# Blockwise causal attention and a ReGLU feed-forward on one core: packed loads and DMA transposes for batches 2 and 3, stores from the ACT queue, a shorter order for batch 0

## The chip, the cores and the metric

The kernel runs on one NeuronCore of a Trainium2 chip. TensorE (PE in the profile) multiplies matrices, VectorE (DVE) and ScalarE (ACT) work on elements, GpSimd (POOL) does so too and issues DMAs, and SyncE (SP) only issues DMAs here. The metric is the device time of one execution in microseconds (us). Ratios are the mean time of one kernel's fast runs over that of the other's fast runs of the same rounds, so they are not quite the ratio of the medians that are quoted. A profile is one execution; its span is about 2 us shorter than the time reported for that execution.

## The reference, cut to what matters

```python
q, k, v: (8 batches, 8 heads, 576 positions, 64), float32
scores = q @ k.T / 8,  masked where block_i < block_j (blocks of 64 positions)
attn   = softmax(scores) @ v
x      = attn with the heads side by side: (8 * 576, 512)
out    = (relu(x @ w_gate) * (x @ w_val)) @ w_out     # d_ff = 1536
```

## The kernel before: the parts that matter

The work is cut into 32 head pairs, r = 0 to 31, four to a batch. For each pair, TensorE makes scores, ACT takes the exponential, TensorE multiplies with v ("av"), and DVE normalises the result into `xnat`. `xnat` is then transposed into `xT`, the input of the feed-forward. The feed-forward is a generator. `ffn(n)` emits its next n matmuls, and these fill the gaps of the attention of later batches. The kernel fixes the order of the instructions of each engine itself, and an instruction that waits holds up those that stand after it in that order.

Batches 0, 1 and 2 are loaded as float32 in packed form (4 x 64 consecutive numbers for a partition), cast to bf16 and transposed by TensorE. The evacuation from PSUM undoes the packing. Batches 3 to 7 are loaded by casting DMAs from POOL and transposed by the DMA engines, with SP issuing the transposes. Stores go out on SP.

```python
def load_qkv(b, which):                       # batches 3 to 7
    ...
            nc.gpsimd.dma_start(dst, src[b, :, 128 * c : 128 * c + n, :].rearrange("h p d -> p h d"))

def dma_transposes(b):
    m, tl = bfs[b, 0], bfs[b, 1]
    for t in range(2):
        nc.sync.dma_start_transpose((qTm, kTm)[t][b % 2]..., m[t]...)
        nc.sync.dma_start_transpose((qTt, kTt)[t][b % 2][:, 0:4, :], tl[t])
...
                ob = sb.tile([128, 512], FP, name="ob", bufs=3)      # end of an output group of ffn
                nc.vector.tensor_copy(ob, op)
                if j < B:
                    r0 = S * j + 128 * s
                    nc.sync.dma_start(out[r0 : r0 + 128, :], ob)
...
        for r in range(4, 4 * B):
            b, hp = divmod(r, 4)
            a = {1: [2, 6, 2, 4], 2: [4, 8, 4, 8]}.get(b, [4, 8, 8, 16])
            ...
            exp_2 = scores_1(r)
            ffn(a[0])
            exp_2()
            if r > 4:
                head_av(r - 1, 0)
                ffn(a[1])
                head_av(r - 1, 1)
                ...                             # xnat transposes: TensorE up to r = 8, DMA after
            if hp == 0 and 2 <= b < B - 1:
                load_qkv(b + 1, (0, 1, 2))
            if hp == 2 and 2 <= b < B - 1:
                dma_transposes(b + 1)
            ffn(a[2])
            scores_2(r)
            scores_3(r)
            if r < 7:
                pe_transposes(1, (r + 1) % 4, e1.m, e1.tl, (dve, dve))
            elif r < 11:
                pe_transposes(2, (r + 1) % 4, e2.m, e2.tl, (dve, dve))
            ffn(a[3])
            corners(r, nc.vector)
```

The softmax here doesn't subtract the row's maximum and nothing guards it: scores larger than these inputs give would overflow.

## Time and profile before

| what | us |
|---|---|
| time, median of the first three runs | 410.58 |
| span of the profiled execution | 406.5 |
| feed-forward begins | 33.10 |
| first scores of batch 3 | 127.30 |
| rest, batch 3 to the end | 279.2 |

The three stretches that these moments bound, in the view by windows of the kernel before. The columns are each engine's busy time with its instruction count, then the granted TensorE clock, the DMA share and the GB/s moved:

```profile
core 0: us, PE busy (x) PEld busy (x) DVE busy (x) ACT busy (x) POOL busy (x), PEclk, DMA share, GB/s
0.00:33.10 33.10, 24.87 (x284) 13.75 (x285) 16.22 (x56) 17.58 (x27) 14.53 (x33) 0.95 1.13 218
33.10:127.30 94.20, 77.20 (x685) 38.16 (x684) 48.20 (x130) 40.59 (x64) 26.73 (x31) 0.95 1.06 148
127.30:406.50 279.20, 274.32 (x2058) 131.07 (x2058) 114.49 (x282) 110.95 (x166) 41.93 (x50) 0.99 0.63 80
```

The last stretch is full, so what can be gained lies before 127.3 us. The longest waits of TensorE in the kernel before, as total, number of times and longest one:

```profile
PE sc L236 <- DMA kTm_89<-k_bf: 9.0, 1, 9.0
PE ffnp L322 <- DVE xnat L305: 4.0, 5, 0.9
PE ffnp L403 <- POOL ident masks.py:199: 1.8, 1, 1.8
PE ffnp L220 <- DVE q_bt L153: 1.7, 1, 1.7
```

The first line is one wait, for the DMA transpose of batch 3's keys. SP issued that transpose at 115.65 us and it landed 11.6 us later. The granted clock is 0.53 between 120 and 130 us. SP's timeline has it (start, duration of the issue, what):

```profile
115.65 5.91 SPq L189 DMA_TRANSPOSE kTm_89<-k_bf  x1
```

### The profile page before, as it was taken

To read this page: it belongs to the slowest core of one execution; us is meant where nothing else is said; L and a number is where in the kernel's file an instruction comes from. 1 tells how busy PE (TensorE), PEld (TensorE's weight loads), DVE (VectorE), ACT (ScalarE), POOL (GpSimd) and SP (SyncE) were. 2 spreads that over 40 slices of the span, in tenths; PEclk is the share of its full clock that TensorE was granted. 3 is DMA by queue.
4 is the path that set the end of the run, shared out by engine and by line. 5 is a ranking of instruction groups with operands and counts; after the bars stand their busy time and mean duration, and the time that the engine had idled before them with its cause. 6 is when DMAs were issued, how large, how long until landed. Compare 5 with 4: busy or idle time off the path is not lost.

```text
span 406.5 us, 7570 instructions
## 1 busy us (share of the span) xinstructions
PE 376.4 (93%) x3024; PEld 183.0 (45%) x3024; DVE 178.9 (44%) x468; ACT 169.1 (42%) x257; POOL 83.2 (20%) x114
## 2 busy tenths in 40 slices
PE   6789898879964999999999999999999999999995
PEld 2444344534432444444445444444444444444442
DVE  2653565476531344444543444344434542433432
ACT  5563255535442345534553555355435511311310
POOL 5710211831340830092019002100000000000000
PEclk9989989999995999999999999999999999999998
DMA  8999996997398996299629962918031012002004
GB/s 206 244 203 240 199 261 169 115 117 59 33 152 82 108 184 103 60 137 175 118 29 172 142 126 31 151 42 131 18 103 32 16 40 77 2 26 79 0 9 95
DMA packets 144274, 43.54 MB, mean 107 GB/s; under 512 B 127856, under 2 KB 139632, under 8 KB 144240
## 3 DMA queue, kind: packets, MB, share of 16 engines
q0 software_dynamic: 76128, 13.57, 44.4%
q1 hardware_dynamic: 68112, 29.51, 32.5%
q8 instruction: 23, 0.38, 0.4%
q14 instruction: 11, 0.09, 0.1%
HBM read 37.75 MB, written 9.44 MB: 116 GB/s over the span
## 4 chain that ended last, share of the span: by engine, by line
PE 83%; DVE 7%; DMA 4%; issue 1%; SPq 1%; ACT 1%; POOL 1%; DVEq 0%; ACTq 0%
PE ffnp L357 23%; PE ffnp L373 22%; PE ffnp L345 22%; PE sc L236 7%; PE av L295 7%; DMA kTm_89<-k_bf 3%; DVE xnat L305 1%; DVE qTm_86 L221 1%; DMA stage<-in_k_dram 1%; PE ffnp L217 1%; DVE hT L367 1%; PE ffnp L322 1%; DVE k_bf L145 1%; DVE q_bf L145 1%; DMA k_bf<-in_k_dram 1%
## 5 line engine op out<-in xcount | busy, mean ns | idle before, releaser
L367 DVE TENSOR_TENSOR hT<-gate_sb,ffnp 128x512 bf16<-128x512 bf16 x108 | 74.2, 687 | 117.5 <-PE ffnp L357 84.2
L354 ACT ACTIVATE gate_sb<-ffnp 128x512 bf16<-128x512 f32 x108 | 64.3, 595 | 86.3 <-PE ffnp L345 85.4
L373 PEld LDWEIGHTS <-hT 128*128 128x128 bf16 x432 | 39.0, 98 | 43.5 <-issue 1.7
L383 DVE COPY ob<-ffnp 128x512 f32<-128x512 f32 x36 | 24.9, 691 | 59.5 <-PE ffnp L373 57.6
L373 PE MATMUL ffnp<-wo_85,hT 128*128 128x512 bf16 x144 | 37.4, 380 | 0.0
L373 PE MATMUL ffnp<-wo_84,hT 128*128 128x512 bf16 x144 | 37.3, 379 | 0.0
L373 PE MATMUL ffnp<-wo_83,hT 128*128 128x512 bf16 x144 | 37.2, 380 | 0.0
L261 ACT ACTIVATE attnT_95<-sc 128x1024 bf16<-128x1024 f32 x16 | 16.4, 1026 | 35.6 <-PE sc L236 31.6
L305 DVE TENSOR_TENSOR xnat<-av,recip 128x320 bf16<-128x320 f32 x60 | 29.5, 492 | 2.1
L251 ACT ACTIVATE attnT_94<-sc 128x1024 bf16<-128x1024 f32 x16 | 16.4, 1025 | 32.8 <-PE sc L236 24.4
L357 PE MATMUL ffnp<-xT,wv_82 128*128 128x512 bf16 x96 | 26.6, 400 | 0.0
L261 ACT ACTIVATE attnT_94<-sc 128x1024 bf16<-128x1024 f32 x16 | 16.4, 1024 | 23.9 <-PE sc L236 23.9
L251 ACT ACTIVATE attnT_95<-sc 128x1024 bf16<-128x1024 f32 x16 | 16.4, 1025 | 23.2 <-PE sc L236 22.0
L345 PE MATMUL ffnp<-xT,wg_78 128*128 128x512 bf16 x96 | 25.2, 383 | 0.3 <-DVE hT L367 0.3
L357 PE MATMUL ffnp<-xT,wv_81 128*128 128x512 bf16 x96 | 24.7, 380 | 0.4 <-DVE qTt_90 L225 0.4
L357 PE MATMUL ffnp<-xT,wv_79 128*128 128x512 bf16 x96 | 24.7, 380 | 0.4 <-DVE qTt_90 L225 0.4
L357 PE MATMUL ffnp<-xT,wv_80 128*128 128x512 bf16 x96 | 24.7, 379 | 0.4 <-DVE qTt_90 L225 0.4
L345 PE MATMUL ffnp<-xT,wg_75 128*128 128x512 bf16 x96 | 24.8, 379 | 0.0
L179 POOL DMA_DIRECT2D v_bf_97<-in_v_dram x15 | 12.6, 856 | 59.5 <-PE av L295 53.1
L345 PE MATMUL ffnp<-xT,wg_76 128*128 128x512 bf16 x96 | 24.7, 380 | 0.0
L345 PE MATMUL ffnp<-xT,wg_77 128*128 128x512 bf16 x96 | 24.7, 380 | 0.0
L295 PEld LDWEIGHTS <-attnT_95 128*128 128x128 bf16 x480 | 19.4, 101 | 10.6 <-DVE xnat L305 2.1
(115 smaller groups left out, 452.1 us busy)
## 6 DMA issues: line engine op xcount, KB each, us to landing
out_dram<-ob SPq DMA_DIRECT2D x32, 256.0 KB, 2.9
stage<-in_v_dram SPq DMA_DIRECT2D x27, 128.0 KB, 5.3
q_bf<-in_q_dram POOLq DMA_DIRECT2D x20, 128.0 KB, 6.3
k_bf<-in_k_dram POOLq DMA_DIRECT2D x20, 128.0 KB, 8.0
stage<-in_q_dram SPq DMA_DIRECT2D x4, 512.0 KB, 5.2
stage<-in_k_dram SPq DMA_DIRECT2D x4, 512.0 KB, 6.2
v_bf_97<-in_v_dram POOLq DMA_DIRECT2D x12, 128.0 KB, 5.1
stage<-in_q_dram SPq DMA_DIRECT2D x4, 256.0 KB, 4.1
```

The costliest lines, as they stand in the source:

```text
L179: nc.gpsimd.dma_start(dst, src[b, :, 128 * c : 128 * c + n, :].rearrange("h p d -> p h d"),)
L236: nc.tensor.matmul(o, kTm[b % 2][ps, c, hp, :] if c < 4 else kTt[b % 2][ps, hp : hp + 2, :].rearrange("p h n -> p (h n)"), qTm[b % 2][ps, ...
L251: nc.scalar.activation(at[:, :, 0:512], sc, AF.Exp, scale=scale)
L261: nc.scalar.activation(at[:, :, 1024:1536], sc, AF.Exp, scale=scale)
L295: nc.tensor.matmul(av[:, p, :], at[:, hh, col : col + 128], vb[:, c, h, :], start=(p == 0), stop=(c == p), skip_group_check=True,)
L305: nc.vector.tensor_tensor(out=xnat[:, :, 64 * hh : 64 * hh + 64], in0=av[:, :, 0:64], in1=recip.to_broadcast([128, NCH, 64]), op=AX.mult,)
L345: nc.tensor.matmul(gate, wg[i][:, c, fo : fo + 128], x[:, c, :], start=(c == 0), stop=(c == 3),)
L354: nc.scalar.activation(gate_sb, gate, AF.Relu)
L357: nc.tensor.matmul(val, wv[i][:, c, fo : fo + 128], x[:, c, :], start=(c == 0), stop=(c == 3),)
L367: nc.vector.tensor_tensor(out=h, in0=gate_sb, in1=val, op=AX.mult)
L373: nc.tensor.matmul(op, hT[f][:, 128 * s : 128 * (s + 1)], wo[f // 4][:, f % 4, :], start=(f == 0), stop=(f == 11),)
L383: nc.vector.tensor_copy(ob, op)
```

## The change: intent and diff

The change makes batch 3's operands early, so that the 9 us wait goes. It also takes transposes off TensorE. Batch 3 gets packed loads too. Batches 2 and 3, and the second half of batch 1, are transposed by DMA into a buffer `perm`, and a copy undoes the packing. POOL does the casts of batches 2 and 3. The 48 matmuls `ffn(8)+ffn(8)+ffn(32)` stand before batch 2. The loads of w_out come later, and those of q and k from batch 4 on earlier. Stores move to ACT and are issued one output group late. Batch 0's loop is reordered.

```diff
+        def transpose(self, hg):
+            for t in range(2):
+                pm = sb.tile([128, 4, 2, 128], BF, name="perm", bufs=8)
+                nc.sync.dma_start_transpose(pm..., self.m[t][:, 1024 * hg : 1024 * hg + 1024])
+        def unpermute(self, hp, engs):          # perm -> qTm, kTm
+            for t in range(2):
+                engs[t]((qTm, kTm)[t][self.b % 2][:, :, hp, :]..., self.perm[t, hp // 2]...)
...
+    def put(j, s, ob):
+            nc.scalar.dma_start(out[r0 : r0 + 128, :], ob)
...
-                    nc.sync.dma_start(out[r0 : r0 + 128, :], ob)
+                if store:
+                    store.pop()()
+                store.append(lambda j=j, s=s, ob=ob: put(j, s, ob))
...
-            a = {1: [2, 6, 2, 4], 2: [4, 8, 4, 8]}.get(b, [4, 8, 8, 16])
+            a = {1: [2, 4, 2, 4], 2: [4, 4, 4, 4]}.get(b, [4, 8, 8, 16])
             if r == 8:
+                head_av(7, 0)
+                ffn(8)
+                head_av(7, 1)
+                ffn(8)
+                to_xT_pe(7)
+                e2.unpermute(0, (dve, pool))
+                ffn(32)
...
+            elif r == 6:
+                e2.transpose(0)
+                e2.transpose(1)
+                e2.transpose_tails()
+                e3 = Early(3, 4)
+                e3.load_qk(0)
+                e3.load_qk(4)
+                e3.load_v(0)
+                e3.load_v(4)
+            elif r == 8:
+                e2.cast_v(0, pool)
+                e2.cast_v(4, pool)
+                e3.cast_qk(0, (pool, pool))
+                e3.cast_qk(4, (pool, pool))
+                e3.transpose(0)
+                e3.transpose(1)
+                e3.transpose_tails()
+            if 8 <= r < 11:
+                e2.unpermute(r - 7, (dve, pool if r == 8 else dve))
+            elif 11 <= r < 15:
+                e3.unpermute(r - 11, (dve, dve))
+            if r == 11:
+                for h0 in (0, 4):
+                    e3.cast_v(h0, pool)
```

(Cut: batch 0's loop; batch 1's start; the loads of q and k from batch 4 on; later places for the transposes of `xnat`; shapes of views.)

More of the change, by code (lines that the diff above doesn't have):

```diff
@@ L90, in new_bf @@
     def new_bf():
-        m = [sb.tile([128, 4, 512], BF, name=n, bufs=2) for n in ("q_bf", "k_bf")]
+        m = [sb.tile([128, 2048], BF, name=n, bufs=2) for n in ("q_bf", "k_bf")]
         t = [sb.tile([64, 512], BF, name=n, bufs=2) for n in ("q_bt", "k_bt")]
@@ L105, in __init__, with load_qk @@
             self.st = {}
-        def load(self, h0, gate=None):
+            self.perm = {}
+        def load_qk(self, h0, gate=None):
             b, per = self.b, self.per
@@ L123, in load, with load_v @@
                 both = new_stage(1024)
-                self.st_t = [both[:, 0:512], both[:, 512:1024], new_stage(512)]
+                self.st_t = [both[:, 0:512], both[:, 512:1024], None]
                 self.tail(0, q)
                 self.tail(1, k)
+            return i
+        def load_v(self, h0, gate=None):
+            b, per = self.b, self.per
             st = self.st[2, h0] = new_stage(256 * per)
             for h in range(per):
-                nc.sync.dma_start(
+                i = nc.sync.dma_start(
                     st[:, 256 * h : 256 * h + 256].rearrange("p (c d) -> p c d", c=4),
@@ L132, in load @@
                 )
+                after(i, gate)
             if h0 == 0:
+                self.st_t[2] = new_stage(512)
                 self.tail(2, v)
@@ L140, in tail, with half, cast_qk @@
             )
-        def cast_qk(self, h0, engs):
+        def half(self, t, hg):
+            return self.m[t][:, 1024 * hg : 1024 * hg + 1024].rearrange(
+                "p (j n) -> p j n", j=4
+            )
+        def cast_qk(self, h0, engs, tails=True):
             per = self.per
+            lo = 64 * (h0 % 4)
             for t in range(2):
                 engs[t](
-                    self.m[t][:, :, 64 * h0 : 64 * (h0 + per)].rearrange(
+                    self.half(t, h0 // 4)[:, :, lo : lo + 64 * per].rearrange(
                         "p j (h d) -> p h j d", d=64
@@ L150, in cast_qk, with cast_tails @@
                 )
-            if h0 == 0:
-                for t in range(2):
-                    engs[t](self.tl[t], self.st_t[t][0:64])
+            if h0 == 0 and tails:
+                self.cast_tails(engs)
+        def cast_tails(self, engs):
+            for t in range(2):
+                engs[t](self.tl[t], self.st_t[t][0:64])
         def cast_v(self, h0, eng):
@@ L165, in cast_v, with transpose_tails, pe_mains, pe_tails @@
                 )
+        def transpose(self, hg):
+            for t in range(2):
+                pm = sb.tile([128, 4, 2, 128], BF, name="perm", bufs=8)
+                nc.sync.dma_start_transpose(
+                    pm.rearrange("p j h n -> p (j h) n"),
+                    self.m[t][:, 1024 * hg : 1024 * hg + 1024],
+                )
+                self.perm[t, hg] = pm
+        def transpose_tails(self):
+            for t in range(2):
+                nc.sync.dma_start_transpose(
+                    (qTt, kTt)[t][self.b % 2][:, 0:4, :], self.tl[t]
+                )
+        def unpermute(self, hp, engs):
+            for t in range(2):
+                engs[t](
+                    (qTm, kTm)[t][self.b % 2][:, :, hp, :].rearrange(
+                        "p c (n j) -> p c n j", j=4
+                    ),
+                    self.perm[t, hp // 2][:, :, hp % 2, :].rearrange(
+                        "p j (c n) -> p c n j", c=4
+                    ),
+                )
+        def pe_mains(self, hp, evac):
+            for t in range(2):
+                tp = psum_ffn.tile([128, 512], BF, name="ffnp")
+                src = self.half(t, hp // 2)
+                lo = 128 * (hp % 2)
+                for j in range(4):
+                    nc.tensor.transpose(
+                        tp[:, 128 * j : 128 * j + 128], src[:, j, lo : lo + 128], ident
+                    )
+                evac[t](
+                    (qTm, kTm)[t][self.b % 2][:, :, hp, :].rearrange(
+                        "p c (n j) -> p c n j", j=4
+                    ),
+                    tp.rearrange("p (j c n) -> p c n j", j=4, c=4),
+                )
+        def pe_tails(self, evac):
+            tp = psum_ffn.tile([128, 2, 4, 64], BF, name="ffnp")
+            for t in range(2):
+                for hp in range(4):
+                    nc.tensor.transpose(
+                        tp[:, t, hp, :],
+                        self.tl[t][:, 128 * hp : 128 * hp + 128],
+                        ident[:64, :64],
+                    )
+            for t in range(2):
+                evac[t]((qTt, kTt)[t][self.b % 2][:, 0:4, :], tp[:, t])
     def load_qkv(b, which):
@@ L176, in load_qkv @@
                         bfs[b, 0], bfs[b, 1] = new_bf()
-                    dst = bfs[b, 0][t][:, c, :] if c < 4 else bfs[b, 1][t]
+                    dst = bfs[b, 0][t][:, 512 * c : 512 * c + 512] if c < 4 else bfs[b, 1][t]
                     dst = dst.rearrange("p (h d) -> p h d", h=8)
@@ L190, in dma_transposes @@
                 (qTm, kTm)[t][b % 2].rearrange("p c h n -> p (c h) n"),
-                m[t].rearrange("p c n -> p (c n)"),
+                m[t],
             )
@@ L209, in load_w_out @@
         return after(ins, gate)
-    def pe_transposes(b, hp, m, tl, evac):
-        hs = slice(128 * hp, 128 * hp + 128)
-        for t in range(2):
-            tp = psum_ffn.tile([128, 1024], BF, name="ffnp")
-            for j in range(4):
-                nc.tensor.transpose(
-                    tp[:, 128 * j : 128 * j + 128], m[t][:, j, hs], ident
-                )
-            nc.tensor.transpose(tp[:, 512:576], tl[t][:, hs], ident[:64, :64])
-            evac[t](
-                (qTm, kTm)[t][b % 2][:, :, hp, :].rearrange("p c (n j) -> p c n j", j=4),
-                tp[:, 0:512].rearrange("p (j c n) -> p c n j", j=4, c=4),
-            )
-            evac[t]((qTt, kTt)[t][b % 2][:, hp, :], tp[:, 512:576])
     def scores(b, hp, pieces):
@@ L273, in corners @@
         at = attnT[r % 2]
-        for c in (0, 512, 896, 1024):
-            eng.memset(at[64:128, :, c : c + 64], 0.0)
+        three = at[64:128, :, 0:1536].rearrange("p g (c n) -> p g c n", c=3)
+        eng.memset(three[:, :, :, 0:64], 0.0)
+        eng.memset(at[64:128, :, 896:960], 0.0)
     xnats = {}
@@ L334, in to_xT_dma @@
         nc.sync.dma_start_transpose(xTt[:, hp, b : b + 1, :], xnat[0:64, 4, :])
+    store = []
+    def put(j, s, ob):
+        if j < B:
+            r0 = S * j + 128 * s
+            nc.scalar.dma_start(out[r0 : r0 + 128, :], ob)
+        else:
+            for i in range(2):
+                r0 = S * (2 * s + i) + 512
+                nc.scalar.dma_start(out[r0 : r0 + 64, :], ob[64 * i : 64 * i + 64])
     def ffn_gen():
@@ L383, in ffn_gen @@
                 nc.vector.tensor_copy(ob, op)
-                if j < B:
-                    r0 = S * j + 128 * s
-                    nc.sync.dma_start(out[r0 : r0 + 128, :], ob)
-                else:
-                    for i in range(2):
-                        r0 = S * (2 * s + i) + 512
-                        nc.sync.dma_start(out[r0 : r0 + 64, :], ob[64 * i : 64 * i + 64])
+                if store:
+                    store.pop()()
+                store.append(lambda j=j, s=s, ob=ob: put(j, s, ob))
                 yield
@@ L410 @@
         for h0 in range(0, 8, 2):
-            e0.load(h0)
+            e0.load_qk(h0)
+            e0.load_v(h0)
         junk(12)
-        e0.cast_qk(0, (dve, act))
-        pe_transposes(0, 0, e0.m, e0.tl, (dve, act))
-        e0.cast_qk(2, (dve, dve))
-        for h0 in range(0, 4, 2):
-            e0.cast_v(h0, pool)
+        e0.cast_qk(0, (dve, act), tails=False)
+        e0.pe_mains(0, (dve, act))
+        e0.cast_tails((dve, dve))
+        e0.cast_v(0, pool)
+        e0.cast_v(2, pool)
         w_in = [load_w_in(i) for i in range(4)]
-        w_out = [load_w_out(i) for i in range(3)]
-        e1 = Early(1, 4)
         for r in range(4):
-            scores_1(r)()
+            exp_2 = scores_1(r)
+            if r == 0:
+                e0.pe_tails((dve, dve))
+            exp_2()
+            if r > 0:
+                head_av(r - 1, 0)
             if r < 3:
-                pe_transposes(0, r + 1, e0.m, e0.tl, (dve, dve))
+                e0.cast_qk(2 * r + 2, (dve, dve))
+                e0.pe_mains(r + 1, (dve, dve))
             if r > 0:
-                corners(r - 1, nc.vector)
-                head_av(r - 1, 0)
-            if r < 2:
-                e0.cast_qk(2 * r + 4, (dve, dve))
+                head_av(r - 1, 1)
+            junk(2)
+            scores_2(r)
+            scores_3(r)
+            junk(3)
+            if r > 0:
+                to_xT_pe(r - 1)
             if 1 <= r < 3:
                 e0.cast_v(2 * r + 2, dve)
-            junk(2)
-            scores_2(r)
-            if r > 0:
-                head_av(r - 1, 1)
-            scores_3(r)
-            junk(2)
-            if r > 0:
-                to_xT_pe(r - 1)
-        e1.load(0, w_in[2])
-        e1.load(4)
-        corners(3, nc.vector)
+            corners(r, nc.vector)
+        e1 = Early(1, 4)
+        e1.load_qk(0, w_in[2])
+        e1_qk = e1.load_qk(4)
         head_av(3, 0)
@@ L446 @@
         to_xT_pe(3)
-        e2 = Early(2, 4)
-        ffn(64)
-        e1.cast_qk(0, (dve, dve))
+        ffn(52)
+        w_out = [load_w_out(i, e1_qk) for i in range(3)]
+        e1.load_v(0)
+        e1.load_v(4)
+        e1.cast_qk(0, (dve, act))
+        ffn(8)
+        e1.pe_mains(0, (dve, dve))
+        e1.pe_tails((dve, act))
+        e1.cast_qk(4, (dve, act))
+        e1.transpose(1)
+        e2 = Early(2, 4)
+        e2.load_qk(0)
+        e2.load_qk(4)
+        e2.load_v(0)
+        e2.load_v(4)
+        ffn(8)
+        e1.pe_mains(1, (dve, dve))
         e1.cast_v(0, pool)
@@ L452 @@
         ffn(8)
-        pe_transposes(1, 0, e1.m, e1.tl, (dve, dve))
-        e2.load(0, w_out[1])
-        e2.load(4)
-        ffn(4)
         for r in range(4, 4 * B):
             b, hp = divmod(r, 4)
-            a = {1: [2, 6, 2, 4], 2: [4, 8, 4, 8]}.get(b, [4, 8, 8, 16])
+            a = {1: [2, 4, 2, 4], 2: [4, 4, 4, 4]}.get(b, [4, 8, 8, 16])
             if r == 8:
-                for h0 in (0, 4):
-                    e2.cast_qk(h0, (dve, dve))
+                head_av(7, 0)
+                ffn(8)
+                head_av(7, 1)
+                ffn(8)
+                to_xT_pe(7)
+                e2.unpermute(0, (dve, pool))
+                ffn(32)
             exp_2 = scores_1(r)
@@ L465 @@
             exp_2()
-            if r > 4:
+            if r in (4, 8):
+                ffn(a[1])
+            else:
                 head_av(r - 1, 0)
@@ L469 @@
                 head_av(r - 1, 1)
-                if r <= 8:
-                    to_xT_pe(r - 1)
-                else:
+                if r > 8:
                     to_xT_dma(r - 1)
-            else:
-                e1.cast_qk(4, (dve, dve))
-                ffn(a[1])
-            if r == 8:
-                for h0 in (0, 4):
-                    e2.cast_v(h0, pool)
-            if hp == 0 and 2 <= b < B - 1:
-                load_qkv(b + 1, (0, 1, 2))
-            if hp == 2 and 2 <= b < B - 1:
-                dma_transposes(b + 1)
+            if r == 4:
+                e1.unpermute(2, (pool, pool))
+                e1.unpermute(3, (pool, pool))
+                e2.cast_qk(0, (pool, pool))
+                e2.cast_qk(4, (pool, pool))
+            elif r == 6:
[20 more added lines that the diff above has]
+            if r == 11:
+                for h0 in (0, 4):
+                    e3.cast_v(h0, pool)
+            if b >= 2 and hp == 2 and b + 2 < B:
+                load_qkv(b + 2, (0, 1))
+            if b >= 3 and b + 1 < B:
+                if hp == 0:
+                    load_qkv(b + 1, (2,))
+                if hp == 2:
+                    dma_transposes(b + 1)
             ffn(a[2])
+            if 4 < r < 8:
+                to_xT_pe(r - 1)
             scores_2(r)
             scores_3(r)
-            if r < 7:
-                pe_transposes(1, (r + 1) % 4, e1.m, e1.tl, (dve, dve))
-            elif r < 11:
-                pe_transposes(2, (r + 1) % 4, e2.m, e2.tl, (dve, dve))
             ffn(a[3])
@@ L497 @@
         ffn(10**6)
+        store.pop()()
 _INS = ['q', 'k', 'v', 'moe_w_gate', 'moe_w_val', 'moe_w_out']
```

## The prediction

> **What bounds the kernel now.** TensorE. It is busy 376.4 of 406.5 us (busy table), 83% of the chain that ended last. But the three parts of the span differ (windows and TensorE timeline):
> - 0 to 33.1 us, attention of batch 0: 24.9 us busy, latency bound. A head pair takes 4.8 to 7.3 us; DVE and TensorE take turns.
> - 33.1 to 127.3 us: feed-forward matmuls of four take 0.866 us (0.2165 each); one head pair's attention costs about 2.0 us, as (39.24 us period of a batch later - 144 x 0.2165)/4. By these this part holds 228 x 0.2165 + 8 x 2.0 + 6 us of transposes = 71 us of work, and takes 94. The waits: 9.0 us in one piece at 118 to 127 for the DMA transpose of batch 3's keys (landed 11.6 us after issue), 4.0 us before the transposes of xnat, 1.7 us on a cast, 1.3 us on evacuations (0.42 us each). The granted clock is halved for 3.4 us twice before 60 us and for 10 us around the long wait (0.53 between 120 and 130). The Trainium skill ("TensorE: Matmul & The Clock Gate", Part 1) says that an idle window of about 3.4 us halves the clock; this trace agrees.
> - 127.3 us to the end: full (201.8 of 202 us busy, then tail). Nothing to gain there.
>
> **What the change does.**
> 1. Batch 3 is loaded early in packed form and cast on Pool, so the 9.0 us wait goes, and with it about 1.8 us of half clock.
> 2. 56 fewer TensorE transposes: about 3 us at 0.055 us each. Evacuations of 0.69 + 0.18 us per tensor leave DVE; SBUF copies (estimated 0.35 to 0.6 us, from the 128x512 casts' 0.41 to 0.62) come in.
> 3. Fillers replace waits: xnat transposes come later, 48 feed-forward matmuls stand before batch 2. 236 instead of 228 are done before batch 3: 1.7 us less afterwards.
> 4. Shorter batch 0: tails off the first chain (0.8 us), head 0's av before the next transposes, one fewer evacuation per tensor: 3 us in all, feed-forward starts near 30 us.
> 5. Stores on ACT, a group late: SP no longer holds loads behind stores. Worth little by itself.
>
> **New costs.** w_out now is asked for after batch 1's q and k (about 37 us); 3 MB took 13 us in before under similar load, and it is needed near 53 us: 0 to 3 us wait. Batch 2's second key copy stands on Pool behind batch 3's casts, whose loads stand on SP behind batch 2's transposes (1.9 to 3.8 us issue for 128x2048): 2 to 5 us wait in batch 2's second head pair. Between the two av of a pair only 4 matmuls (0.87 us) remain against a normalising of about 1.0 us: 0.2 us x 7.
>
> **Sum.** 30 + 71 + about 9 of waits to the start of batch 3 (110 us), then 1060 x 0.2165 + 20 x 2.0 + 4.7 tail = 275 us: span 385. Times stand 2 to 4 us over the span: 388 us, range 380 to 397. Nearly all is on the critical path. Faster 0.95, same 0.04, slower 0.01.
>
> **What would show it.** Feed-forward start near 30; batch 3's first scores near 110 with no long DMA wait; the period after that still 39.2 us per batch; the largest new wait at batch 2's second head pair, on Pool.
>
> **What would make it wrong.** Pool or w_out much later than estimated , or ACT stores delaying Relu in the full part.

## The result, and the profile after

The changed kernel takes 396.01 us (median of 4 runs, 395.18 to 397.32) against 410.17 us for the kernel before on the same chip. The ratio is 0.966, with a 95% interval of 0.962 to 0.970. That lies inside the predicted range of 380 to 397, close to its upper end. The central forecast of 388 was 8 us too good: a gain of about 22 us was expected and 14 came.

The same three stretches in the view by windows of the changed kernel:

```profile
core 0: us, PE busy (x) PEld busy (x) DVE busy (x) ACT busy (x) POOL busy (x), PEclk, DMA share, GB/s
0.00:31.30 31.30, 23.49 (x283) 13.77 (x288) 15.82 (x44) 16.71 (x25) 12.41 (x30) 0.95 1.15 221
31.30:117.50 86.20, 73.08 (x624) 35.22 (x635) 41.71 (x85) 43.28 (x69) 35.70 (x40) 0.98 1.33 201
117.50:393.90 276.40, 269.41 (x2012) 129.52 (x2049) 117.35 (x250) 109.90 (x166) 42.22 (x50) 1.00 0.72 82
```

The first stretch is 1.8 us shorter, the second 8.0 us and the last 2.8 us. In the last, 1.7 us are the 8 matmuls that are now done earlier. The middle stretch was forecast at 80 us, from 30 to 110, and took 86.2. TensorE's longest waits in the changed kernel:

```profile
PE ffnp L217 <- DVE q_bf L159: 3.8, 3, 1.3
PE ffnp L427 <- ACT gate_sb L424: 2.9, 1, 2.9
PE sc L294 <- DVE kTm_88 L202: 2.1, 1, 2.1
PE ffnp L469 <- POOL ident masks.py:199: 1.8, 1, 1.8
PE ffnp L217 <- DVE hT L437: 1.4, 1, 1.4
PE av L354 <- DVE xnat L364: 1.4, 3, 0.5
```

The 9 us wait is gone. Two new waits stand near the place of batch 2, and neither is the one that was forecast.

**The first of them: ACT stands behind a store.** ACT's instructions around 82 us in the changed kernel, from the timeline (start, duration, what; in brackets the idle time before, and what ended it):

```profile
80.20 0.58 ACT L383 COPY xT<-ffnp 128x512 bf16<-128x512 bf16 x1 [5.16 <-PE ffnp L382]
80.68 0.22 ACT L384 COPY xTt<-ffnp 128x64 bf16<-128x64 bf16 x1
85.61 0.34 ACTq L401 DMA_DIRECT2D out_dram<-ob  x1
85.99 1.09 ACT L424 ACTIVATE gate_sb<-ffnp 128x512 bf16<-128x512 f32 x2 [5.09 <-DMA stage<-in_k_dram]
```

The store at 85.61 writes an output tile that DVE had finished at 78.34. What ended ACT's wait was a load of keys. On POOL, the cast of that key load begins at 85.68, which is the same moment (POOL's timeline):

```profile
85.68 1.04 POOL L159 CAST k_bf<-stage 128x1024 bf16<-128x1024 f32 x1 [1.36 <-DMA stage<-in_k_dram]
```

Every Relu of the feed-forward stands behind this store on ACT, so TensorE waits 2.9 us (83.7 to 86.6 us), and its clock is halved for 3.4 us after that (86.8 to 90.3 us). In the compiled program each DMA from SP or ACT, but for the first eight, waits first for one of eight completion counters, which SP and ACT share in turn. The lines for that store and for the last DMA before it that holds the same counter (from the list of compiled instructions, not the profile):

```
SP   DMACopy stage_1039<-in_k_dram 128x4x256 [waits DMAHW3_49]
ACT  DMACopy out_0_dram<-ob_1215 128x512     [waits DMAHW3_49,DVE_49]
```

So a store on ACT waits for the landing of an unrelated load that SP issued. This is the first theory to test.

**The second: a copy of 3.09 us.** DVE near 102 us in the changed kernel, from the timeline:

```profile
101.28 3.09 DVE L202 COPY qTm_86<-perm 128x512 bf16<-128x512 bf16 x1
104.30 0.58 DVE L202 COPY kTm_88<-perm 128x512 bf16<-128x512 bf16 x1
```

POOL at the same time:

```profile
101.26 1.12 POOL L174 CAST v_bf_97<-stage 128x1024 bf16<-128x1024 f32 x1
102.25 0.69 POOL L179 CAST v_bf_97<-stage 64x512 bf16<-64x512 f32 x1
102.80 1.12 POOL L174 CAST v_bf_97<-stage 128x1024 bf16<-128x1024 f32 x1
```

Two copies of one form take 3.09 and 0.58 us. The long one spans three POOL casts and ends 0.45 us after the last of them. The Trainium skill ("SBUF — State Buffer", section "SBUF: two separate sides") says that DVE and GpSimd share a pair of SBUF ports as an exclusive lock, held for a whole instruction. This is the second theory.

### The profile page after: what moved, and what is told of

It reads as the page before. It is cut to its first block, busy times and chain, and to the rows that moved or that the text cites. A ratio compares the mean times of both kernels' runs of the same rounds, so it can differ in the third digit from the quotient of the medians.

```text
span 393.9 us, 7338 instructions
## 1 busy us (share of the span) xinstructions
PE 366.0 (93%) x2918; PEld 178.5 (45%) x2972; DVE 174.9 (44%) x378; ACT 169.9 (43%) x259; POOL 90.3 (23%) x120
## 4 chain that ended last, share of the span: by engine, by line
PE 74%; issue 2%; ACT 2%; DVE 2%; DMA 2%; SPq 1%; ACTq 0%; DVEq 0%
PE ffnp L443 22%; PE ffnp L427 21%; PE ffnp L415 19%; PE av L354 6%; PE sc L294 6%; DMA stage<-in_k_dram 2%; DVE xnat L364 1%; ACT attnT_94 L319 1%; ACT attnT_95 L319 1%; DVE hT L437 1%; ACT gate_sb L424 1%; SPq L196 0%; DVE ob L453 0%; DVE recip L363 0%; SPq L117 0%
## 5 line engine op out<-in xcount | busy, mean ns | idle before, releaser
L443 PE MATMUL ffnp<-wo_84,hT 128*128 128x512 bf16 x139 | 36.6, 380 | 0.3
L443 PE MATMUL ffnp<-wo_83,hT 128*128 128x512 bf16 x139 | 35.9, 379 | 0.4
L443 PE MATMUL ffnp<-wo_85,hT 128*128 128x512 bf16 x133 | 35.1, 380 | 0.4
L427 PE MATMUL ffnp<-xT,wv_79 128*128 128x512 bf16 x96 | 25.6, 390 | 2.9 <-ACT gate_sb L424 2.9
L415 PE MATMUL ffnp<-xT,wg_75 128*128 128x512 bf16 x95 | 25.6, 390 | 0.1
L363 DVE RECIPROCAL recip<-av 128x5 f32<-128x5 f32 x60 | 11.5, 192 | 30.6 <-PE av L354 30.6
L427 PE MATMUL ffnp<-xT,wv_82 128*128 128x512 bf16 x93 | 24.8, 380 | 0.2
L415 PE MATMUL ffnp<-xT,wg_77 128*128 128x512 bf16 x95 | 24.5, 380 | 0.4 <-issue 0.2
L427 PE MATMUL ffnp<-xT,wv_81 128*128 128x512 bf16 x89 | 24.3, 379 | 0.6 <-DVE kTm_89 L220 0.2
L415 PE MATMUL ffnp<-xT,wg_78 128*128 128x512 bf16 x95 | 24.6, 379 | 0.1
L415 PE MATMUL ffnp<-xT,wg_76 128*128 128x512 bf16 x88 | 23.5, 380 | 0.4
L427 PE MATMUL ffnp<-xT,wv_80 128*128 128x512 bf16 x91 | 23.6, 379 | 0.0
L354 PEld LDWEIGHTS <-attnT_94 128*128 128x128 bf16 x480 | 18.6, 99 | 9.5 <-DVE xnat L364 2.8
```

The source lines that it names most:

```text
L354: nc.tensor.matmul(av[:, p, :], at[:, hh, col : col + 128], vb[:, c, h, :], start=(p == 0), stop=(c == p), skip_group_check=True,)
L363: nc.vector.reciprocal(recip, av[:, :, 64])
L415: nc.tensor.matmul(gate, wg[i][:, c, fo : fo + 128], x[:, c, :], start=(c == 0), stop=(c == 3),)
L427: nc.tensor.matmul(val, wv[i][:, c, fo : fo + 128], x[:, c, :], start=(c == 0), stop=(c == 3),)
L443: nc.tensor.matmul(op, hT[f][:, 128 * s : 128 * (s + 1)], wo[f // 4][:, f % 4, :], start=(f == 0), stop=(f == 11),)
```

## The experiments

Twelve runs were made, the first of them a repeat. Unless said otherwise, each alters only the named part of the changed kernel. The milestones and the span are from one profiled execution, which need not be a typical one: that of x1_tails_first was the fastest of its four (388.81 us), that of x9_pool_stores the fastest of its four (402.48) and that of x12_all_cast the fastest of its six (389.88, the others 393.05 to 393.40). In us:

| run | time, median | ratio to before | feed-forward begins | batch 2's first scores | batch 3's first scores | span |
|---|---|---|---|---|---|---|
| before | 410.17 | 1 | 33.10 | 82.22 | 127.30 | 406.5 |
| after | 396.01 | 0.966 | 31.31 | 91.87 | 117.52 | 393.9 |
| c0_after_again | 395.78 | 0.966 | 30.55 | 92.58 | 117.37 | 393.8 |
| x1_tails_first | 390.15 | 0.951 | 30.23 | 86.36 | 110.45 | 386.8 |
| x2_castv_act | 394.02 | 0.962 | 31.99 | 91.81 | 115.85 | 392.2 |
| x3_qtail_act | 395.48 | 0.965 | 30.48 | 92.66 | 118.69 | 395.3 |
| x4_sp_stores | 408.57 | 0.996 | 32.05 | 103.39 | 127.02 | 408.5 |
| x5_before_act_stores | 410.15 | 1.000 | 33.67 | 82.41 | 129.54 | 409.9 |
| x6_batch3_plain | 397.46 | 0.968 | 30.51 | 90.23 | 117.44 | 396.2 |
| x7_old_batch0 | 396.45 | 0.964 | 32.19 | 92.77 | 117.45 | 393.9 |
| x9_pool_stores | 406.35 | 0.992 | 31.80 | 87.79 | 112.37 | 400.7 |
| x10_two_late | 396.04 | 0.967 | 31.58 | 92.71 | 117.48 | 393.9 |
| x11_all | 391.18 | 0.956 | 31.42 | 87.22 | 112.58 | 389.0 |
| x12_all_cast | 393.23 | 0.958 | 30.29 | 87.09 | 111.59 | 388.0 |

(The changed kernels do 172 feed-forward matmuls before batch 2's first scores and the kernel before 132, so that column compares only among kernels of one kind.)

### Control: the changed kernel again

> The changed kernel once more, unaltered, as the control that the next three runs are compared with on the same chip. Expected: span 393.5 to 395.5 us, ratio to the kernel before 0.962 to 0.970, and the same three stalls: ACT's third output store issued near 85.6 us with TensorE waiting 2.9 us for gate_sb; one 128x512 copy of batch 2's queries of about 3.1 us on DVE near 101 us; one 64x512 cast of 2.3 us on DVE near 43 us.

It took 395.78 us (5 runs, 395.29 to 396.14). ACT's late store and the 2.9 us wait came back. The long DVE copy took 2.23 us this time, and TensorE's wait for kTm 1.3 us:

```profile
102.00 2.23 DVE L202 COPY qTm<-perm 128x512 bf16<-128x512 bf16 x1
```

The 2.3 us cast near 43 us, which stood behind TensorE's 1.4 us wait for `hT` in the first profile, did not come back; it took 0.60 us. So that third stall is not a property of the kernel but of one execution. In this control ACT's first store (71.87 us) also waited, 3.09 us, for a load of batch 2's v.

### Does the store wait for a shared counter, or for full queues?

In this run the same bytes are loaded in another order, so that the DMA with the store's counter is a small one that lands early.

```diff
-                e3.load_qk(0)                  # q, k mains, then q, k tails
+                e3.load_tails()                # q, k tails
+                e3.load_qk(0, tails=False)     # then the mains
                 e3.load_qk(4)
```

The compiled list now has the key tail as the holder of counter 3:

```
SP   DMACopy stage_1038<-in_k_dram 64x8x64   [waits DMAHW3_49]
ACT  DMACopy out_0_dram<-ob_1215 128x512     [waits DMAHW3_49,DVE_49]
```

> Only the order of batch 3's six q and k loads is changed: the two small tails first, then the four mains. The bytes in flight are the same. In the compiled program the third output store on ACT waits for completion counter 3 of the eight that the DMAs of SP and ACT share in turn; in the changed kernel the last DMA with that counter was batch 3's first 512 KB key load, here it is the 64-row key tail. Theory (shared counter): the store goes when ACT reaches it, about 81 us, instead of 85.6; ACT's wait of 5.1 us falls below 1 us, TensorE's 2.9 us wait for gate_sb and the half clock after it go, span 4 to 5 us shorter (389 to 390). Rival (the store is held because the loads fill the DMA queues): the same bytes are there, so the store still goes near 85 us and the span stays within 1 us of 394.

ACT in this run, from the timeline:

```profile
79.11 0.22 ACT L387 COPY xTt<-ffnp 128x64 bf16<-128x64 bf16 x1
81.72 0.40 ACTq L404 DMA_DIRECT2D out_dram<-ob  x1
82.17 1.08 ACT L427 ACTIVATE gate_sb<-ffnp 128x512 bf16<-128x512 f32 x2 [2.83 <-PE ffnp L418]
```

The store goes at 81.72 instead of 85.61 to 86.32. ACT is idle for 2.83 us before the Relu. The profile puts the end of that down to TensorE, but the trace also records when each counter moves. Read with the compiled lists, the counter of this store reached its value 0.08 us before the store was issued, in all nine profiles that have such a store on ACT behind a load of batch 3's keys (at 85.54 us in the changed kernel, at 81.64 us here). So the store still waited 2.3 us for the key tail (ACT was free at 79.33 us), and the "below 1 us" of the expectation was missed. TensorE's wait for `gate_sb` is 0.7 us instead of 2.9:

```profile
PE ffnp L430 <- ACT gate_sb L427: 0.7, 1, 0.7
```

The clock is not halved before the tail. The median is 390.15 us, 5.6 us below the control, and the intervals of the two ratios do not touch (0.948 to 0.954 against 0.963 to 0.968). The counter theory holds and the theory of full queues falls: the traffic was the same. No kernel of the study has a lower median.

Not all of the 5.6 us are this stall. From the last TensorE transposes of `xnat` before it to batch 2's first scores, the changed kernel takes 12.23 us and the control 12.25, this run 8.28: 4.0 us less. And in this run, by its timing alone, DVE's copies of batch 2 did not meet POOL's casts of v:

```profile
96.75 0.95 DVE L205 COPY kTm<-perm 128x512 bf16<-128x512 bf16 x1
99.82 1.06 POOL L177 CAST v_bf<-stage 128x1024 bf16<-128x1024 f32 x1
```

No copy took more than 0.95 us from there to batch 3, and TensorE's wait for DVE's copy of kTm was gone with the v casts still on POOL. The rest of the difference was not traced.

### The same theory asked the other way: stores later, stores elsewhere

If the store merely stood too early, two groups late would cure it. The counter theory says that it does not, because the counters are dealt out anew and the large key load again holds the store's counter.

```diff
-                ob = sb.tile([128, 512], FP, name="ob", bufs=3)
+                ob = sb.tile([128, 512], FP, name="ob", bufs=5)
-                if store:
-                    store.pop()()
+                if len(store) == 2:
+                    store.pop(0)()
```

> The changed kernel with stores two groups late instead of one, and five output buffers instead of three. Rival of the counter theory: ACT was stuck because the store stood too early, before its data or its queue were ready; then a later store cures it and the span is 389 to 391. Counter theory: the counters are dealt out anew, and in the compiled program the store that ACT now meets at about 81 us waits for counter 2, which batch 3's first 512 KB key load holds; ACT stands until that load lands, near 85 us, as before. Only the earlier wait (for batch 2's v) goes. Span 391 to 395, with TensorE waiting 2 to 4 us for gate_sb.

ACT in this run:

```profile
86.62 0.34 ACTq L401 DMA_DIRECT2D out_dram<-ob  x1
87.01 1.08 ACT L424 ACTIVATE gate_sb<-ffnp 128x512 bf16<-128x512 f32 x2 [5.54 <-DMA stage<-in_k_dram]
```

ACT stood 5.54 us, TensorE waited 3.4 us for `gate_sb`, and the span was 393.9 us (393.9 to 395.5 over the four executions, median 394.0), as the counter theory said. The time is 396.04 us, no different from the control.

The next run issues the stores from POOL, whose DMAs have counters of their own in the compiled list.

```diff
-            nc.scalar.dma_start(out[r0 : r0 + 128, :], ob)
+            nc.gpsimd.dma_start(out[r0 : r0 + 128, :], ob)
```

> The changed kernel with its stores issued from Pool instead of ACT, still one group late. Pool's DMAs have completion counters of their own. Theory (ACT stands because its store waits for a counter shared with SP's loads): no load can hold a store's counter now, ACT's waits of 5.1 us and about 3 us for stage loads are both gone, TensorE's 2.9 us wait for gate_sb goes, span 386 to 390. Rival (what hurts is the store's traffic among the loads, from whatever queue): TensorE still stands 2 to 4 us near 82 to 87 us and the span stays at 392 or more.

Both theories missed the total: 406.35 us. The milestones tell why. Up to batch 3 the run behaves as the counter theory says. ACT waits for no load of batches 2 or 3, TensorE has no wait above 0.82 us between 70 and 93 us, and batch 3 begins at 112.37 us, 5.0 us before the control. After that it loses more than it won, because POOL is one queue in order too. One of POOL's waits in this run:

```profile
POOL v_bf L252 <- PE av L354: 42.3, 2, 21.8
```

And DVE's for output buffers:

```profile
DVE ob L453 <- DMA out_dram<-ob: 19.8, 4, 6.1
```

POOL's loads of a later batch's v must wait until the buffer is free. The stores stand behind them (three went together at 121.66 us), and DVE waits up to 6.1 us for an output buffer. TensorE pays for it where DVE's normalising comes late (1.4 us of this wait in the control):

```profile
PE av L354 <- DVE xnat L364: 9.4, 7, 3.2
```

The stall moved; it did not go away.

### Is the move of the stores worth anything?

The prediction said "worth little by itself". Two runs ask that: the stores back on SP in the changed kernel, and on ACT in the kernel before.

```diff
-            nc.scalar.dma_start(out[r0 : r0 + 128, :], ob)    # changed kernel
+            nc.sync.dma_start(out[r0 : r0 + 128, :], ob)
```

> The changed kernel with its output stores back on the SP queue, still one group late. The prediction called the move to ACT worth little. Theory now: it is what lets the early loads stand in front, because SP is one queue in order: batch 3's loads issue from 77.6 to 93.4 us, and block 0's stores would stand behind them, so the fourth output copy on DVE (three buffers) waits from about 81 to about 96 us, and TensorE behind it. Expected: a wait of 10 to 14 us at 81 to 96 us, half clock after it, span 402 to 412, so most or all of the change's gain is gone. Rival (stores worth little wherever they are): span 389 to 394, faster than the control, as ACT's 5.1 us wait on the shared counter goes.

> The kernel before with only its stores moved to ACT, one group late. There the SP queue holds loads and stores of batch 2 too, but its one wait of DVE for a store is 1.9 us. Worth little by itself: span within 1.5 us of the kernel before (405 to 408). If the shared counter also bites here, ACT's first store waits for a load of batch 2's v and the kernel is 1 to 3 us slower; if SP's order was holding batch 3's transposes, the 9.0 us wait for kTm shrinks and it is 3 us or more faster.

With the stores on SP the changed kernel takes 408.57 us, a ratio of 0.996 to the kernel before, so nearly the whole gain is gone. Its longest TensorE wait:

```profile
PE ffnp L415 <- DVE ob L453: 10.9, 1, 10.9
```

And SP's queue ahead of the stores, from the timeline:

```profile
84.72 5.54 SPq L135 DMA_DIRECT2D stage<-in_v_dram  x4
90.30 1.06 SPq L145 DMA_DIRECT2D stage<-in_v_dram  x1
91.47 2.24 SPq L135 DMA_DIRECT2D stage<-in_v_dram  x4
93.81 1.60 SPq L401 DMA_DIRECT2D out_dram<-ob  x3
```

Three stores stand behind batch 3's loads until 93.81 us. The fourth output copy finds no buffer, and TensorE waits 10.9 us for it. In the kernel before, the same move does nothing: 410.15 against 410.14 us, ratio 1.000, with 8.5 us of wait for batch 3's keys still there:

```profile
PE sc L236 <- DMA kTm<-k_bf: 8.5, 1, 8.5
```

Both halves of the theory hold. The move is worth nothing alone and about 13 us (408.57 - 395.78) once the early loads stand on SP.

### What the packed load of batch 3 brings

```diff
-                e3 = Early(3, 4) ... loads, casts, transposes, unpermute
+                if hp == 0:
+                    load_qkv(b + 1, (0, 1, 2))     # from batch 2 on, as before
+                if hp == 2:
+                    dma_transposes(b + 1)
```

> The changed kernel with batch 3 loaded as in the kernel before: cast loads from Pool asked for at batch 2's start and DMA transposes two head pairs later, no packed load. Claim 1 of the prediction: packing batch 3 removes the 9.0 us wait. Theory: that wait returns in part or whole (4 to 10 us for a DMA transpose of batch 3's keys at batch 3's first scores), but the two stalls that the packed loads brought (ACT's store behind a load, about 5 us with the half clock; DVE beside Pool's v casts, about 2 us) go: span 391 to 399. Rival (the wait came from the stores and loads on SP and not from the way batch 3 is loaded): no wait above 2 us at batch 3 and span 386 to 389.

TensorE at batch 3's first scores in this run:

```profile
117.44 0.61 PE L294 MATMUL sc<-qTm,kTm 64*128 64x512 bf16 x6 [3.69 <-DMA kTm<-k_bf]
```

The wait returns, with 3.7 us instead of 9.0 (4 to 10 had been expected), and ACT's stall on a key load is gone; a stall of 4.8 us on batch 2's v remains in this execution. The time is 397.46 us, 1.7 us above the control of another group of runs (ratios 0.968 and 0.966, intervals overlapping). So as it was, packing batch 3 brings next to nothing net. What it removes, its own loads give back through ACT. With the tails first (390.15 us, in another group of runs) it is worth about 7 us. So most of the 14 us that the change gained was there without the packed load of batch 3. No run undoes batch 2's DMA transposes, the 48 matmuls before batch 2 or the later transposes of `xnat`, so how the gain divides among them stays open.

### DVE beside POOL

Batch 3's three v casts go to ACT:

```diff
-                    e3.cast_v(h0, pool)
+                    e3.cast_v(h0, act)
```

> Only batch 3's three casts of v go from Pool to ACT. Theory (DVE's SBUF to SBUF copy and Pool's instructions take turns at a shared port): the 3.09 us copy of batch 2's queries on DVE near 101 us, which lies over three Pool casts (1.12, 0.69, 1.12 us), is 0.6 us again; TensorE's wait of 2.1 us for kTm goes; span 1.5 to 2.5 us shorter if ACT's 2.7 us of casts hide. Rival (the copy is slow because the DMA transposes of batch 3 write SBUF at the same time, 93 to 106 us): the copy stays near 3 us and the span within 0.7 us of the control.

The two copies in this run, on DVE's timeline:

```profile
101.22 0.59 DVE L202 COPY qTm<-perm 128x512 bf16<-128x512 bf16 x1
101.72 0.59 DVE L202 COPY kTm<-perm 128x512 bf16<-128x512 bf16 x1
```

The copy takes 0.59 us instead of 2.23 (control) or 3.09, TensorE's wait for kTm is gone, and the time is 394.02 us, 1.8 us below the control. The intervals of the two ratios overlap (0.959 to 0.964 and 0.963 to 0.968), so the size is not sharp. The DMA transposes of batch 3 ran at the same time here too, so they alone are not the cause. POOL's casts are: in four profiles (changed kernel, control, x3_qtail_act, x10_two_late) the held copy ended 0.44 or 0.45 us after the last of the three casts, and in the run with the tails first, where copies and casts did not overlap, no copy took over 0.95 us. In a fifth profile (x7_old_batch0) they took turns: the copies took 1.27 and 1.44 us and the last cast 1.52.

The cast near 43 us was the same question for batch 1:

```diff
-        e1.cast_qk(0, (dve, act))
+        e1.cast_qk(0, (dve, act), tails=False)
+        e1.cast_tails((act, act))
```

> Only the 64x512 cast of batch 1's query tail goes from DVE to ACT. Same theory as for the v casts: on DVE it took 2.27 us beside Pool's w_out issue and v casts, against 0.41 to 0.82 us elsewhere. Theory: TensorE's wait of 1.4 us at 44.7 to 46.1 us goes[...], ACT's Relu comes 0.6 us later, span 0.8 to 1.5 us shorter. Rival (TensorE waits there for PSUM buffers that gate and val matmuls hold, whatever the cast): the wait stays above 1 us and the span within 0.5 us.

This one misses. The time is 395.48 us, no different from 395.78. The 1.4 us wait is gone, but it was gone in the control as well, where the cast on DVE took 0.60 us. Whether DVE meets POOL there depends on when a load lands: the w_out issue on POOL began at 40.99, 41.47 and 42.10 us in the three profiles. This execution also lost 4.5 us near 72 us, where ACT's first store waited 5.74 us for batch 2's v, a shared counter at another place, and 2.5 us for kTm, again behind a DVE copy beside POOL's casts (3.46 us).

### Batch 0's order

```diff
-            if r > 0:
-                head_av(r - 1, 0)
-            if r < 3:
-                e0.cast_qk(2 * r + 2, (dve, dve))
-                e0.pe_mains(r + 1, (dve, dve))
-            if r > 0:
-                head_av(r - 1, 1)
...
+            if r < 3:
+                e0.pe_mains(r + 1, (dve, dve))   # its casts one round earlier
+            if r > 0:
+                corners(r - 1, nc.vector)
+                head_av(r - 1, 0)
...
```

> The changed kernel with batch 0's loop in the order of the kernel before (next transposes before the av, one more cast ahead, corners later); the tails stay off the first chain. The prediction gave the whole shorter order 3 us, and the feed-forward began 1.8 us earlier (31.3 against 33.1). Theory: about 1 us of that is the loop's order: feed-forward start 32.0 to 33.0, span 0.7 to 2 us over the control. Rival: the order brings nothing and all 1.8 us come from the tails and the missing w_out loads: start 31.3, span within 0.5 us.

It took 396.45 us (392.45 to 397.8). The feed-forward begins at 32.19 us, but it begins anywhere from 30.23 to 32.05 us in the ten profiles with the new order, so one profile can't tell. The times don't tell the kernels apart either. What the loop's order brings stays open; it is at most about 2 us.

### The cures together

> Three cures together: small tails first in batch 3's loads, batch 3's v casts on ACT, stores two groups late. Each alone gave 5.6 us (tails first) and 1.8 us (v casts); the two-late stores should take off the 1 to 3 us of the first store's wait for batch 2's v. The tails hold the store's counter here too. Expected: 386.5 to 389 us, no ACT wait for a stage load above 1 us, no half clock between 20 us and the end.

> As the run with three cures, and in batch 0's loop the casts of the next head pair's q and k stand before the normalising of the last one on DVE, not after it. TensorE waits 3.2 to 3.8 us in three places for these casts now. Expected: these waits fall to 1 us or less, part comes back as waits for the normalising; feed-forward start 1 us earlier, total 0.5 to 1.5 us below the run with three cures. If DVE is simply full in batch 0, no difference (within 0.5 us).

The first joins the tails first, the v casts on ACT and the two-late stores. The second also puts batch 0's casts before the normalising on DVE. They took 391.18 us (386.5 to 389 had been expected) and 393.23 us (it was to be 0.5 to 1.5 us below the first), so neither beats the tails alone at 390.15. One reason lies in the profile of that run: DVE's copies met no POOL casts there anyway, so moving the v casts had nothing left to cure. Between batch 1's first scores (52.14 us) and batch 2's (87.22 us) the joint run needs 35.1 us, against 36.6 with the tails alone, so the later stores do something. It lost that and more at the start (31.42 against 30.23 us for the feed-forward) and in batch 2. ACT's store and the Relu behind it in the run with three cures:

```profile
82.44 0.34 ACTq L404 DMA_DIRECT2D out_dram<-ob  x1
82.83 0.60 ACT L427 ACTIVATE gate_sb<-ffnp 128x512 bf16<-128x512 f32 x1 [1.82 <-DMA stage<-in_k_dram]
```

And in the run with the earlier casts as well:

```profile
82.51 0.34 ACTq L404 DMA_DIRECT2D out_dram<-ob  x1
82.89 1.09 ACT L427 ACTIVATE gate_sb<-ffnp 128x512 bf16<-128x512 f32 x2 [4.25 <-DMA stage<-in_k_dram]
```

A wait of at most 1 us had been expected. ACT was free at 81.01 and 78.65 us, and the store went at 82.44 and 82.51. SP had issued the key tail 3.15 and 3.37 us before that (2.94 us in the run with the tails alone). So the store keeps step with the landing of the load that holds its counter (0.08 us after it in both), and arriving there earlier only makes ACT wait longer. With the casts before the normalising, TensorE waits 2.5 us for batch 0's query casts instead of 3.9, and the feed-forward begins at 30.29 us, inside the range that the other kernels show. No gain in the total can be seen, and what made five of the six executions over 3 us slower than the profiled one is not in this profile.

## Why the prediction was right or wrong

- **The total.** The time lies within the range (one of the four executions, 397.32 us, lies just outside). The forecast gain was 22 us and the measured one 14, so the centre was too optimistic. That it lies in the range is in part luck: two stalls, together 6.1 us, were not in the sum, and the two new waits that it named for w_out and for batch 2's second head pair came to nothing in this kernel.
- **"Batch 3 is loaded early in packed form and cast on Pool, so the 9.0 us wait goes."** Right as to the wait. As to its net worth, wrong in this version: without the packing the time is only about 1.7 us longer (not told apart), since its loads stall ACT.
- **"feed-forward starts near 30 us".** 31.3 in the first profile, 30.2 to 32.1 over ten profiles with the new order. The size was about right.
- **"30 + 71 + about 9 of waits to the start of batch 3 (110 us)".** This is the term that was mis-sized. Batch 3 began at 117.5, and 117.5 - 31.3 - 71 leaves 15 us of waits and half clock. The six too many are, by the traces, the ACT stall (4.0 us against the run that shortens it) and TensorE's 2.1 us wait for kTm, behind a DVE copy that the prediction had put at 0.35 to 0.6 us and that took 3.09 beside POOL's casts (0.59 without them). In the run with the tails first, which escaped both, batch 3 begins at 110.45 us.
- **"2 to 5 us wait in batch 2's second head pair", on Pool.** Wrong. There was no such wait in the changed kernel: POOL's late key copy was done at 92.77 us and the second pair's scores began at 96.62. A wait of 2.1 us came one pair later, from DVE, whose copy could not run beside POOL's casts. The forecast wait was hidden behind the ACT stall: where that stall is gone or shorter, the second pair does wait for POOL's key copy, 0.57 us with the tails first, 1.07 us with the stores on POOL and 1.43 us with three cures. Its size was too large all the same.
- **"w_out ... 0 to 3 us wait".** None was seen, the low end of that range.
- **"0.2 us x 7" between the two av.** It was 0.45 to 0.46 us, three times, in batch 2: 1.4 us. The sum agrees by chance, from another size and count.
- **"Stores on ACT ... Worth little by itself."** True to the letter (ratio 1.000 in the kernel before) and misleading in substance. It is worth 13 us in the changed kernel, and it brings the largest stall. The prediction looked at ACT's room to issue stores and not at what each store waits for.
- **The period after batch 3.** 39.35 us per batch (127.32 to 166.67) against 39.24. Right.
- **"What would make it wrong ... ACT stores delaying Relu in the full part."** The right danger in the wrong place: Relu was delayed, but before the full part, while large loads were in flight.

## What to carry to other kernels

Ask of every DMA instruction what its queue waits for before it issues, counters handed out by the compiler included. A store that shares a counter with a large load is a wait for that load, and on a compute engine's queue it stops that engine's arithmetic (here ACT's, for 5.1 us). Moving a stream from one in-order queue to another moves the question of what stands behind what: here the stores on SP or POOL cost 13 or 11 us more than on ACT, for two different reasons. And when a change gains less than forecast, look at the engine that feeds TensorE, not at the operand that the change was meant to bring earlier.

## What the Trainium skill lacked or had wrong

- "DMA: Bandwidth & Descriptors", section "Issuing engines are not separate DMA queues", says that issuing from several engines "will only save the time on the sequencer it takes to initiate the DMA". Here the issuing engine of the stores made the time 408.57 us (SP), 406.35 us (POOL) or 395.78 us (ACT), because waits in an in-order queue hold all that stands behind them. The sentence is about the transfers, and it leaves this out.
- The same page, section "Why a DMA increments its semaphore by 16 and not by 1", advises one semaphore per in-flight slot. It does not say what sharing costs across queues: ACT stood 5.1 us with an output store that waited for a load issued by SP, and batch 2's first scores came 4.0 us earlier, counted from the last transposes before the stall, when a small load held the counter.
- "SBUF — State Buffer", section "SBUF: two separate sides", has the port lock held for one instruction, by DVE only in a two-port mode or with two SBUF inputs. The lock agrees with the runs: a bf16 copy of 512 elements for a partition took 0.59 us without POOL's casts and 1.3 to 3.5 us beside them. Whether that copy ran in a two-port mode the traces do not tell. What the page does not say is that a held copy can wait out several POOL instructions in a row: in four of five profiles it ended only 0.44 or 0.45 us after the last of three casts.
- "TensorE: Matmul & The Clock Gate", Part 1, has the clock halved "after ≥1 idle window (~3.4µs)". The length agrees: the half clock lasted 3.41 us after the stall in the changed kernel and 10.24 us, three times that, around the 9 us wait in the kernel before. The idle time does not: the clock was also halved where the longest wait was 1.7 us (kernel before, near 51 us) or 2.9 us (changed kernel, near 85 us).
